# Seven block products of a pair of chunks, 512 columns each, in three single banks

## The chip, the cores and the metric

One core of a Trainium2 chip runs the whole program. The metric is the device time of one launch in microseconds (us), as the median of several runs.

## The reference

```python
B, N, C = 4, 6080, 256                       # q, k, v: (B, N, C); d_ff = 2048
qn = q / (np.linalg.norm(q, axis=1, keepdims=True) + 1e-06)
kn = k / (np.linalg.norm(k, axis=1, keepdims=True) + 1e-06)
s = kn.transpose(0, 2, 1) @ qn / tau         # (B, 256, 256): attention over channels
s = s - s.max(-1, keepdims=True)
a = np.exp(s)
a /= a.sum(-1, keepdims=True) + 1e-09
x = (v @ a).reshape(B * N, C)                # 24320 tokens
h = x @ w_in                                 # 256 -> 2048
g = np.where(h > 0.0, h, np.exp(np.minimum(h, 0.0)) - 1.0)
out = g @ w_out                              # 2048 -> 256
```

The weights arrive as float64; v and the output are stored with channels first.

## The kernel before

Since `(v a) w_in = v (a w_in)`, the kernel works out `a w_in` (256 x 2048) once per batch and multiplies the columns of v (tokens) by it. Every factor of a matmul is held as two fp32r tiles, a high part ("hi", a rounded copy) and a low part ("lo", the exact value minus hi), and a product is three matmuls: hi x hi, hi x lo, lo x hi. A batch has 12 chunks of tokens, 8 of 512 columns and 4 of 496.

Batch 0 runs in an older loop (one matmul set per 128 rows of h, `h_item`, `elu`, `out_item`). Beside it batch 1 is prepared. From chunk 12 (`NB`) on, which is the stretch of the change, the work goes in 144 units `(c, fq)`: chunk c and a quarter fq of the 2048 rows of h (512 rows). A unit multiplies a 2 x 2 block matrix A (the quarter of `a w_in`) by the 2 x 2 block matrix B (the chunk of v: two halves of the channels by two halves of the columns) with seven products instead of eight (Winograd's form). The sums of A blocks (S1 to S4) are made once per batch and quarter (`plan_s`), the sums of B blocks (T1 to T4) once per chunk (`t_sum`, `t_hi`, `t_lo`; `b_hi` and `b_lo` for the plain blocks B11, B21, B22). `product` issues one of the seven: both halves j of 128 rows, 3 matmuls each, 256 (or 248) columns, both halves into one PSUM bank of 512 columns.

In a unit PE goes: A11 x B11 into bank_a; S3 x T3 into bank_e; S2 x T2, later S1 x T1 and S4 x B22 into bank_b, on top of what lies there; A12 x B21 on top of bank_a; A22 x T4 on top of bank_e. Between them ACT copies bank_a into bank_b and bank_e into an SBUF tile p7, and DVE adds bank_b to p7, once into bank_e and once into p7. So four quads of h come about (e11 in bank_a, e21 in bank_e, e22 in p7, e12 in bank_b). For each of them ACT does Relu and Exp (`relu_exp`, L1183 and L1184), DVE a maximum (`largest`, L1187), the hi part goes out by a rounding DMA of POOL's queue (`hi_part`, L1204; for e12 by ACT, L1202), and in the next unit DVE makes the lo part (`lo_parts`, L1210 and L1212). With these parts `multiply_out` does the second product: three matmuls of the chunk's columns (L1127 to L1129, "out matmuls") for each half of the 256 output rows, added up in two po banks over the chunk's 16 row blocks, one or two units later. `copy_out` has ACT copy a full po bank and SP store it.

bank_a and bank_e come from a ring of three PSUM banks, bank_b is a fixed one, two banks are po, and two ("gram") hold what is prepared for the next batch.

From batch 2 on, the preparation of the batch runs beside the units, in small tasks: rows of q and k are loaded by SP, hi parts come by DMA from POOL, lo parts by DVE, squares by ACT, a DMA of POOL adds the squares up (acc), and PE adds to the channel product q, k ("gram", two matmuls a row and half, L203 and L210, one after each out matmul). Then follow norms, softmax, `a w_in` and the S sums.

The order on all five engines is written out: PE, ACT, DVE, POOL and SP are on a manual schedule, and each instruction waits for semaphores in its queue's order. Tasks sit in lists by engine and level. At fixed places of a unit, `spend(engine, budget, now)` takes ready tasks from these lists until their costs, in us, have used the budget; a task is ready when its time `when` (4 steps a unit) has come and what it needs lies some steps back (`late`, `GAP`).

Of the kernel before, what the change touches and what calls it, by code (L numbers as in the profile page):

```python
# [54 lines left out]
def channel_attention_then_elu_ffn(ctx: ExitStack, tc, q, k, vT, tau, w_in, w_out, outT):  # L55
# [33 lines left out]
    WB = 3  # L89
# [105 lines left out]
    def gram_item(hl, gram, ct, first, last):  # L195
# [6 lines left out]
        for r in range(2):  # L202
# [13 lines left out]
            )  # L216

# [554 lines left out]

# [16 lines left out]
    def new_s(fq):  # L789
        s_tiles[fq] = work.tile([P, 2, SPARE + 1, HF], F32R, tag="wp", bufs=2 * KT, name=f"s_{fq}")  # L790
# [54 lines left out]
    s_tiles = {}  # L845
# [104 lines left out]
    queues = {(e, level): [] for e in (ACT, DVE, POOL, PE, SP) for level in range(-2, 4)}  # L950
    GAP = {ACT: 0, DVE: 0, POOL: 2, PE: 2, SP: 0}

    class Task:
# [14 lines left out]
    def task(engine, cost, fn, deps=(), when=0, level=1, late=None):  # L968
# [3 lines left out]
        t.cost = cost  # L972
# [3 lines left out]
    def spend(engine, budget, now):  # L976
        for level in range(-2, 4):
            queue = queues[engine, level]
            while True:
# [7 lines left out]
                t.done = now  # L987

# [32 lines left out]
    def t_sum(c, k):
        hn = half_of(c)
        if k == 0:
            state["tt", c] = work.tile([P, 4, HF], F32, tag="raw", bufs=5, name=f"tt_{c}")
        v = vraw[c][:, :, 0 : 2 * hn].rearrange("p k (x t) -> p k x t", x=2)
        tt = state["tt", c][:, :, 0:hn]
        (
            lambda: nc.vector.tensor_sub(tt[:, 0:2], v[:, :, 1], v[:, 0]),
            lambda: nc.vector.tensor_add(tt[:, 2], tt[:, 1], v[:, 0, 0]),
            lambda: nc.vector.tensor_sub(tt[:, 3], v[:, 1, 0], tt[:, 2]),  # L1030
        )[k]()

# [4 lines left out]
    def t_lo(c, k):
        hn = half_of(c)
        t = t_groups[c % 2][:, k : k + 2]
        nc.vector.tensor_sub(t[:, :, 1, 0:hn], state["tt", c][:, k : k + 2, 0:hn], t[:, :, 0, 0:hn].bitcast(F32))  # L1040
        for y in range(2):
            operands[c, TERMS[k + y]] = t[:, y]

    TERMS = ("T1", "T3", "T2", "T4")

    BLOCKS = (("B11", 0, 0), ("B21", 1, 0), ("B22", 1, 1))

    def block_of(c, k):
        name, kt, x = BLOCKS[k]
        hn = half_of(c)  # L1050
        ring = (3 * (c - NB) + k) % FQ
        return s_tiles[ring][:, :, SPARE], vraw[c][:, kt, x * hn : (x + 1) * hn], hn, name

    def b_hi(c, k):
        to, _, hn, _ = block_of(c, k)
        _, kt, x = BLOCKS[k]
        t0 = span(c)[1] + x * hn
        nc.gpsimd.dma_start(to[:, 0, 0:hn], vT[kt * P : kt * P + P, t0 : t0 + hn])

    def b_lo(c, k):  # L1060
        to, src, hn, name = block_of(c, k)
        nc.vector.tensor_sub(to[:, 1, 0:hn], src, to[:, 0, 0:hn].bitcast(F32))
        operands[c, name] = to
# [527 lines left out]
```

## Time and profile before

| | |
|---|---|
| median of 3 runs | 2115.5 us (2113.42 to 2115.95) |
| the profiled execution's own time | 2112.71 us |
| its span, first to last instruction | 2110.9 us |
| PE busy | 2099.6 us, 99% of the span |
| DVE busy | 1594.0 us, 76% |
| ACT busy | 1475.1 us, 70% |
| POOL busy | 394.9 us, 19% |
| granted TensorE clock | 1.0 of full speed throughout |

In the rows of the timeline the columns are start and duration in us, engine, line, operation, out<-in, shape and count; in groups they are the busy time in us, the mean duration in ns, and the idle time of the engine just before, with what ended it. A row of waits reads: engine and instruction that waited, what it waited for, us in total, times, longest. Rows of windows have for each engine the busy time and count, then granted clock, DMA share and GB/s. Busy times of PE overlap: a matmul's duration goes past the start of the next one.

### The profile page before, as it was taken

To read this page: it belongs to the slowest core of one execution; us is meant where nothing else is said; L and a number is where in the kernel's file an instruction comes from. 1 tells how busy PE (TensorE), PEld (TensorE's weight loads), DVE (VectorE), ACT (ScalarE), POOL (GpSimd) and SP (SyncE) were. 2 spreads that over 40 slices of the span, in tenths; PEclk is the share of its full clock that TensorE was granted. 3 is DMA by queue.
4 is the path that set the end of the run, shared out by engine and by line. 5 is a ranking of instruction groups with operands and counts; after the bars stand their busy time and mean duration, and the time that the engine had idled before them with its cause. 6 is when DMAs were issued, how large, how long until landed. Compare 5 with 4: busy or idle time off the path is not lost. (4 is left out here: it accounts for less than half of the span.)

```text
span 2110.9 us, 35013 instructions
## 1 busy us (share of the span) xinstructions
PE 2099.6 (99%) x12833; PEld 1932.3 (92%) x12833; DVE 1594.0 (76%) x2428; ACT 1475.1 (70%) x2524; POOL 394.9 (19%) x715
## 2 busy tenths in 40 slices
PE   9999999999999999999999999999999999999999
PEld 8888888899889999999999999999999999999998
DVE  7988677777877777777778777777877877777775
ACT  6887776767776776777667767667766766766765
POOL 0000000000013333322122333332222221122211
PEclk9999999999999999999999999999999999999999
DMA  9320222220358787854456887876445443433432
GB/s 355 121 80 26 77 70 70 70 70 30 112 167 225 217 223 209 237 157 132 127 181 209 224 217 214 227 206 173 134 139 175 141 122 105 129 117 105 129 100 95
DMA packets 163371, 312.27 MB, mean 148 GB/s; under 512 B 17408, under 2 KB 59520, under 8 KB 161664
## 3 DMA queue, kind: packets, MB, share of 16 engines
q0 software_dynamic: 101376, 191.00, 32.8%
q1 hardware_dynamic: 61680, 118.91, 17.0%
q8 instruction: 102, 1.67, 0.3%
q14 instruction: 69, 0.57, 0.1%
q10 hardware_dynamic: 144, 0.13, 0.0%
HBM read 134.33 MB, written 31.20 MB: 78 GB/s over the span
## 5 line engine op out<-in xcount | busy, mean ns | idle before, releaser
L1127 PE MATMUL po<-g,wo 128*128 128x512 f32 (+1 forms) x1158 | 438.9, 379 | 0.0
L1129 PE MATMUL po<-g,wo 128*128 128x512 f32 (+1 forms) x1158 | 437.0, 377 | 0.0
L1128 PE MATMUL po<-g,wo 128*128 128x512 f32 (+1 forms) x1158 | 437.0, 377 | 0.0
L1204 POOL DMA_DIRECT2D g<-held x288 | 154.5, 536 | 930.4 <-DVE held L1187 511.9
L1183 ACT ACTIVATE held<-bank_a 128x512 f32<-128x512 f32 (+1 forms) x144 | 85.3, 592 | 324.3 <-PE po L1128 131.5
L1184 ACT ACTIVATE held<-held 128x512 f32<-128x512 f32 (+1 forms) x432 | 270.5, 626 | 13.8
L1212 DVE TENSOR_TENSOR g<-held,g 128x1024 fp32r<-128x1024 f32 (+1 forms) x216 | 260.3, 1205 | 24.1 <-DMA g<-held 24.1
L1104 PEld LDWEIGHTS bank_b<-t,s 128*128 128x128 f32 x1728 | 234.7, 191 | 24.8 <-ACT bank_b L1497 10.0
L1104 PE MATMUL bank_b<-t,s 128*128 128x256 f32 (+1 forms) x1728 | 240.6, 275 | 6.2 <-ACT bank_b L1497 5.8
L1129 PEld LDWEIGHTS po<-g,wo 128*128 128x128 f32 x1158 | 218.9, 189 | 28.9 <-DVE g L1212 0.5
L1104 PE MATMUL bank_e<-t,s 128*128 128x256 f32 (+1 forms) x1728 | 240.0, 275 | 0.0
L1128 PEld LDWEIGHTS po<-g,wo 128*128 128x128 f32 x1158 | 220.2, 190 | 17.3
L1127 PEld LDWEIGHTS po<-g,wo 128*128 128x128 f32 x1158 | 220.7, 191 | 13.0
L1505 DVE TENSOR_TENSOR bank_e<-bank_b,p 128x512 f32<-128x512 f32 (+1 forms) x144 | 99.7, 692 | 154.6 <-PE bank_b L1104 75.2
L1104 PEld LDWEIGHTS bank_e<-t,s 128*128 128x128 f32 x1728 | 216.1, 192 | 0.0
L1513 DVE TENSOR_TENSOR p<-bank_b,p 128x512 f32<-128x512 f32 (+1 forms) x144 | 98.8, 686 | 112.7 <-PE bank_b L1104 112.6
L1104 PE MATMUL bank_a<-s,s 128*128 128x256 f32 (+1 forms) x1296 | 179.8, 275 | 0.0
L1104 PEld LDWEIGHTS bank_a<-s,s 128*128 128x128 f32 x1296 | 168.2, 192 | 4.6
L114 ACT CAST g<-e 128x512 fp32r<-128x512 f32 (+1 forms) x192 | 116.7, 608 | 70.8 <-DVE e L447 39.4
L115 DVE TENSOR_TENSOR g<-e,g 128x512 fp32r<-128x512 f32 (+1 forms) x192 | 131.2, 683 | 46.2 <-ACT g L114 44.8
L474 PE MATMUL po<-g,wo 128*128 128x512 f32 (+1 forms) x378 | 142.7, 377 | 0.0
L472 PE MATMUL po<-g,wo 128*128 128x512 f32 (+1 forms) x378 | 142.6, 377 | 0.0
(228 smaller groups left out, 4344.9 us busy)
## 6 DMA issues: line engine op xcount, KB each, us to landing
g<-held POOLq DMA_DIRECT2D x192, 256.0 KB, 2.7
g<-other POOLq DMA_DIRECT2D x96, 256.0 KB, 3.8
g<-held POOLq DMA_DIRECT2D x96, 248.0 KB, 2.2
acc<-sq POOLq DMA_DIRECT2D x46, 512.0 KB, 5.0
raw<-in_q_dram SPq DMA_DIRECT2D x76, 256.0 KB, 4.9
raw<-in_k_dram SPq DMA_DIRECT2D x76, 256.0 KB, 5.3
v<-in_v_dram SPq DMA_DIRECT2D x32, 512.0 KB, 4.7
out_dram<-o SPq DMA_DIRECT2D x56, 256.0 KB, 2.0
```

Of the source, the lines that this page charges most:

```text
L114: nc.scalar.copy(hi, src)
L115: nc.vector.tensor_sub(lo, src, hi.bitcast(F32))
L472: nc.tensor.matmul(o, wo[:, f, 1, ds], hi, start=False, stop=False)
L474: nc.tensor.matmul(o, wo[:, f, 0, ds], lo, start=False, stop=last(c, f))
L1104: nc.tensor.matmul(bank[:, j, 0:hn], w[:, x, js], y, start=(begin and j == 0 and k == 0), stop=(j == 1 and k == 2), skip_group_check=True,)
L1127: yield nc.tensor.matmul(o, wo[:, f, 0, ds], hi, start=begin, stop=False)
L1128: yield nc.tensor.matmul(o, wo[:, f, 1, ds], hi, start=False, stop=False)
L1129: yield nc.tensor.matmul(o, wo[:, f, 0, ds], lo, start=False, stop=end)
L1184: nc.scalar.activation(e, e, AF.Exp, scale=-1.0)
L1204: nc.gpsimd.dma_start(to, e)
L1212: nc.vector.tensor_sub(lo, held[:, row, :, 0 : 2 * hn], hi.bitcast(F32))
L1505: nc.vector.tensor_add(ve, vb, vp)
```

## The change

A unit is now `(p, fq, j)`: a pair p of chunks, a quarter fq, and one of the two 128-row halves j of each A block. The two column halves of B are the two chunks of the pair. So a product is three matmuls of 512 (or 496) columns in one bank, and a unit makes 256 rows of h for two chunks where it made 512 rows for one. The number of units, 18 x 4 x 2 = 144, is as before, and so are the number of quads in a unit (four of 512 columns) and of out matmuls (24).

```diff
-    def product(bank, c, fq, a, t, begin=False):
-        hn = half_of(c)
-        w, m = s_tiles[fq][:, :, MATRICES.index(a)], operands[c, t]
-        hi, lo = (in_turns(m[:, x, 0:hn]) for x in range(2))
-        for j in range(2):
-            js = slice(j * P, j * P + P)
-            for k, (x, y) in enumerate(((0, hi), (0, lo), (1, hi))):
-                nc.tensor.matmul(bank[:, j, 0:hn], w[:, x, js], y, ...)
+    def product(bank, p, fq, j, a, t, begin=False):
+        n = columns(p)[1]
+        w = s_tiles[fq][:, :, MATRICES.index(a), j * P : j * P + P]
+        hi, lo = (in_turns(x[:, 0:n]) for x in operands[p, t])
+        for k, (x, y) in enumerate(((0, hi), (0, lo), (1, hi))):
+            nc.tensor.matmul(bank[:, 0:n], w[:, x], y, start=(begin and k == 0), stop=(k == 2), skip_group_check=True)
+        if (fq, j) == (FQ - 1, 1):
+            room.extend(operands.pop((p, t)))
...
+    bank_a, bank_e = (ps.tile([P, CH], F32, tag="w", bufs=WB, name=f"bank_{x}") for x in "ae")
...
+    PACE = PERIOD * 25 / NG          # was PERIOD * 30 / NG
...
+        product(bank_a, p, fq, j, "A11", "B11", True)
+        nc.scalar.copy(vb, va)
+        used = spend(DVE, 2.7, now)
+        spend(POOL, 3.9, now)
+        product(bank_e, p, fq, j, "S3", "T3", True)
+        nc.scalar.copy(vp, ve)
+        multiply_out(1, now)
+        spend(ACT, -0.3 if turn else 1.1, now)
+        product(bank_b, p, fq, j, "S2", "T2")
+        nc.vector.tensor_add(ve, vb, vp)
+        if before is not None:
+            before[0]()
+        product(bank_a, p, fq, j, "A12", "B21")
+        e11 = new_quad(u, 0, 0)
+        relu_exp(e11, va)
+        multiply_out(1, now + 1)
+        product(bank_e, p, fq, j, "A22", "T4")
+        e21 = new_quad(u, 1, 0)
+        relu_exp(e21, ve)
+        spend(ACT, -0.3, now + 1)
+        largest(e11, va)
+        hi_part(u, 0, 0)
+        product(bank_b, p, fq, j, "S1", "T1")
+        nc.vector.tensor_add(vp, vb, vp)
+        multiply_out(2, now + 1)
...
+        largest(e21, ve)
+        hi_part(u, 1, 0)
+        if before is not None:
+            before[1]()
+        product(bank_b, p, fq, j, "S4", "B22")
+        e12 = new_quad(u, 0, 1)
+        relu_exp(e12, vb)
...
+        multiply_out(2, now + 2)
+        if not turn:
+            largest(e22, vp)
+            hi_part(u, 1, 1)
+        multiply_out(2, now + 3)
+        largest(e12, vb)
+        hi_part(u, 0, 1)
...
+        used += spend(DVE, min(0.3, 3.0 - used), now + 3)
+        spend(ACT, 0.6 if turn else 1.7, now + 3)
```

`before[0]` and `before[1]` are the lo parts of the unit before (`lo_parts`, rows 1 and 0, two DVE instructions each). `turn` is the second unit of a pair, in which ACT copies out the four po banks of the pair before.

The rest, in words. PSUM: bank_a, bank_b and bank_e are fixed banks; four banks are po (two chunks, two halves of the output rows), and one is left for gram, so what is prepared for a batch takes turns in it. All hi parts of quads go by POOL's DMA. The exact v of a pair lies in two tiles; the T sums are made in them in place, and the full po banks are copied into them before the next pair is loaded. The 14 operand tiles of a pair (seven terms, hi and lo) come from a stock of 20: those of the B blocks of the next pair are made early, those of its T terms in the last unit of a pair, when the tiles of the old pair come free (`hi_of` on ACT, `lo_of` on DVE). ACT's and DVE's tasks are taken by due time instead of by level, with due tasks allowed over the budget. Rows of q and k go in halves (256 KB transfers), 24 groups over 25 units' steps instead of 30; gram takes three matmuls of 256 columns (hi x hi, hi x lo, lo x hi) where it took one of 512 and one of 256. The norms are summed per channel in columns and spread by one matmul.

How the instructions stand on PE, at the start of a unit near the end of the program (bank_a, bank_e and bank_b as above, po the out matmuls, g, t and s operand tiles). Before:

```order
L1104 MATMUL bank_a<-s_4777,s_4971 128x248 x6
L1104 MATMUL bank_e<-t_4716,s_4971 128x248 x6
L1127 MATMUL po_0_18812<-g_5161,wo 128x496
L1128 MATMUL po_0_18812<-g_5161,wo 128x496
L1129 MATMUL po_0_18812<-g_5224,wo 128x496
L1127 MATMUL po_0_18812<-g_5161,wo 128x496
L1128 MATMUL po_0_18812<-g_5161,wo 128x496
L1129 MATMUL po_0_18812<-g_5224,wo 128x496
L1104 MATMUL bank_b<-t_4716,s_4971 128x248 x6
```

Now, at the same place:

```order
L1145 MATMUL bank_a<-t_5047,s_5105 128x496
L1145 MATMUL bank_a<-t_more,s_5105 128x496
L1145 MATMUL bank_a<-t_5047,s_5105 128x496
L1145 MATMUL bank_e<-g_5177,s_5105 128x496
L1145 MATMUL bank_e<-t_4718,s_5105 128x496
L1145 MATMUL bank_e<-g_5177,s_5105 128x496
L1155 MATMUL po_0_5229<-g_5177,wo 128x496
L1156 MATMUL po_0_5229<-g_5177,wo 128x496
L1157 MATMUL po_0_5229<-g_5108,wo 128x496
L1145 MATMUL bank_b<-t_5047,s_5105 128x496
L1145 MATMUL bank_b<-g_5253,s_5105 128x496
L1145 MATMUL bank_b<-t_5047,s_5105 128x496
```

Three long matmuls stand for six short ones, and one set of out matmuls instead of two stands between S3 and S2, which waits for ACT's copy into bank_b.

On ACT, around that copy (L1497 before, L1567 now), where other and held are tiles of quads. Before:

```order
L1183 ACTIVATE held<-bank_b 128x496
L1184 ACTIVATE held<-held 128x496
L1183 ACTIVATE other_5092<-bank_e 128x496
L1184 ACTIVATE other_5092<-other_5092 128x496
L1202 CAST g_5249<-held 128x496
L1497 COPY bank_b<-bank_a 128x2x248
L1499 COPY p_5094<-bank_e 128x2x248
```

Now:

```order
L1219 ACTIVATE held<-bank_e 128x512
L1220 ACTIVATE held<-held 128x512
L1219 ACTIVATE held<-p_5100 128x512
L1220 ACTIVATE held<-held 128x512
L1219 ACTIVATE other_5103<-bank_b 128x512
L1220 ACTIVATE other_5103<-other_5103 128x512
L1567 COPY bank_b<-bank_a 128x512
L1571 COPY p_5100<-bank_e 128x512
```

Before the copy stood e12 (bank_b), e21 (bank_e) and a cast; now it is e12 alone, with e21 and e22 earlier.

On DVE, a unit from one sum into bank_e (L1505 before, L1575 now) on; p is p7, g the hi and lo parts. Before:

```order
L1505 TENSOR_TENSOR bank_e<-bank_b,p_5094 128x2x248
L1212 TENSOR_TENSOR g_5224<-held,g_5249 128x2x496
L1513 TENSOR_TENSOR p_5094<-bank_b,p_5094 128x2x248
L1187 SCALAR_TENSOR_TENSOR held<-held,bank_a 128x496
L1210 TENSOR_TENSOR g_5224<-other_5092,g_5249 128x496
L1210 TENSOR_TENSOR g_5224<-other_5093,g_5249 128x496
L1187 SCALAR_TENSOR_TENSOR held<-held,p_5094 128x496
```

Now:

```order
L1575 TENSOR_TENSOR bank_e<-bank_b,p_5100 128x512
L1244 TENSOR_TENSOR g_5108<-held,g_5177 128x512
L1244 TENSOR_TENSOR g_5108<-held,t_5107 128x512
L1223 SCALAR_TENSOR_TENSOR other_5104<-other_5104,bank_a 128x512
L1590 TENSOR_TENSOR p_5100<-bank_b,p_5100 128x512
L1223 SCALAR_TENSOR_TENSOR held<-held,bank_e 128x512
L1244 TENSOR_TENSOR g_5108<-other_5102,g_5177 128x512
L1244 TENSOR_TENSOR g_5108<-other_5103,t_5107 128x512
```

The lo parts of row 1 (L1244), which wait for POOL's DMAs, and the maximum of e11 (L1223) now stand ahead of the sum into p7 (L1590); there was one lo part (L1212, of row 0) before.

More of the change, by code (lines that the diff above doesn't have):

```diff
@@ L216, in gram_item, with gram_items @@
             )
+    def gram_items(hl, gram, ct, first, last):
+        cs = slice(ct * P, ct * P + P)
+        for r in range(2):
+            for k, (x, y) in enumerate(((0, 0), (0, 1), (1, 0))):
+                yield nc.tensor.matmul(
+                    gram[:, ct, :],
+                    hl[:, x, 1, r, cs],
+                    in_turns(hl[:, y, 0, r, :]),
+                    start=(first and ct == 0 and r == 0 and k == 0),
+                    stop=(last and r == 1 and k == 2),
+                    skip_group_check=True,
+                )
     def keep_warm(n):
@@ L976, in spend @@
     def spend(engine, budget, now):
-        for level in range(-2, 4):
+        whole = budget
+        if engine in (ACT, DVE):
+            queue = queues[engine, 0]
+            while True:
+                able = [t for t in queue if t.ready(now) and (t.cost <= budget + 0.3 or t.due < (0 if engine == DVE else -15))]
+                if not able:
+                    return whole - budget
+                t = min(able, key=lambda t: t.due)
+                queue.remove(t)
+                budget -= t.cost
+                t.fn()
+                t.done = now
+        for level in range(-4, 4):
             queue = queues[engine, level]
@@ L1037, in t_lo @@
[L1037 to L1052, printed above, removed]
@@ L1330, in plan_rows @@
+            los = [task(DVE, 1.22, lo, ready, due=t + 4 + 4.8 * g, late=3 if n == 2 else 0)]
+            for y, (square, add) in enumerate(squares):
+                s = task(ACT, 0.57, square, [*los, *([] if g else [prior.get("pw")])], due=t + 4 + 4.8 * g, late=0)
+                added[g, y] = task(POOL, 0.55, add, [s], level=1, late=1) if g else s
             for ct in range(KT):
@@ L1420, in plan_soft @@
-        for cost, fn in ((0.3, guarded), *turns[0], *refining, *turns[1], (0.2, taken)):
-            x = task(DVE, cost, fn, [x], level=0, late=1)
+            n["dg"] = tiny.tile([P, KT, P], F32, tag="y", bufs=1, name="dg")
+            for jt in range(KT):
+                nc.vector.tensor_scalar(n["dg"][:, jt], ident, n["ry"][:, 2 * jt : 2 * jt + 1], None, op0=ALU.mult)
+        x = task(DVE, 0.7, inverted, [x], due=t + 150, late=1)
+        x = task(DVE, 0.5, taken, [x], due=t + 150, late=1)
@@ L1519, in channel_attention_then_elu_ffn @@
-        product(bank_e, c, fq, "A22", "T4")
-        if before is not None:
-            before[2]()
-        relu_exp(e22, vp)
-        largest(e22, vp)
-        hi_part(u, 1, 1, hn)
-        relu_exp(e12, vb)
-        relu_exp(e21, ve)
-        largest(e12, vb)
-        hi_part(u, 0, 1, hn, True)
-        multiply_out(2, now + 2)
-        spend(DVE, 1.4, now + 2)
-        spend(ACT, 0.4, now + 2)
-        spend(POOL, 3.3, now + 2)
-        spend(SP, 1, now + 2)
-        def finish(e21=e21, ve=ve, u=u, hn=hn):
-            largest(e21, ve)
-            hi_part(u, 1, 0, hn)
```

573 lines of the change are left out of this document (308 added, 265 removed).

## The prediction

> **What bounds the kernel now.** I read the page's first lines, then the PE's waits, then the PE in order of time in the last quarter, where nothing but the products and the out matmuls run.
>
> ```profile
> PE 2099.6 (99%) x12833; PEld 1932.3 (92%) x12833; DVE 1594.0 (76%) x2428; ACT 1475.1 (70%) x2524; POOL 394.9 (19%) x715
> PE bank_b L1104 <- ACT bank_b L1497: 5.8, 10, 2.0
> PE bank_b L1104 <- DVE bank_e L1505: 0.4, 2, 0.2
> ```
>
> PE is busy for 99% of the span and waits in the unit stretch 12 times, 6.2 us in all. So time can only go by fewer or shorter matmul slots on PE, and can come back only by new waits of PE. A matmul's busy time overlaps the next one's, so its cost is read from starts. First a unit of a chunk of 512 columns, then one of 496:
>
> ```profile
> 1760.38 0.38 PE L1127 MATMUL po<-g,wo 128*128 128x512 f32 x1
> ...
> 1763.64 0.83 PE L1104 MATMUL bank_b<-s,s 128*128 128x256 f32 x6
> 1764.31 0.83 PE L1104 MATMUL bank_e<-t,s 128*128 128x256 f32 x6
> 1764.98 0.38 PE L1127 MATMUL po<-g,wo 128*128 128x512 f32 x1
> ...
> 1766.28 0.83 PE L1104 MATMUL bank_a<-s,s 128*128 128x256 f32 x6
> ...
> 1768.91 0.83 PE L1104 MATMUL bank_b<-t,s 128*128 128x256 f32 x6
> ...
> 1770.25 0.38 PE L1127 MATMUL po<-g,wo 128*128 128x512 f32 x1
> ```
>
> ```profile
> 2040.02 0.38 PE L1127 MATMUL po<-g,wo 128*128 128x496 f32 x1
> ...
> 2041.28 0.83 PE L1104 MATMUL bank_a<-s 128*128 128x248 f32 x6
> 2041.94 0.83 PE L1104 MATMUL bank_e<-t,s 128*128 128x248 f32 x6
> 2042.61 0.38 PE L1127 MATMUL po<-g,wo 128*128 128x496 f32 x1
> ...
> 2049.73 0.38 PE L1127 MATMUL po<-g,wo 128*128 128x496 f32 x1
> ```
>
> Twelve product matmuls of 256 columns take 1764.98 - 1763.64 = 1.34 us, 111.7 ns each. The unit takes 1770.25 - 1760.38 = 9.87 us and holds 42 of them and 24 out matmuls, so one of 512 columns takes (9.87 - 42 x 0.1117) / 24 = 215.8 ns. With 496 columns: 12 products of 248 take 1.33 us, 110.8 ns each; the unit takes 9.71 us, an out matmul (9.71 - 42 x 0.1108) / 24 = 210.6 ns. A product matmul of 248 columns thus costs nearly what one of 256 does, while the long ones scale with their columns: in a row of short ones something beside the columns takes a share.
>
> **The change, part by part.**
>
> *Products.* 42 short matmuls a unit become 21 long ones with the same columns; there are 144 units before and after, 96 of 512 columns and 48 of 496. 512: 42 x 111.7 - 21 x 215.8 = 4691 - 4532 = 0.16 us a unit, 15.3 us. 496: 42 x 110.8 - 21 x 210.6 = 4654 - 4423 = 0.23 us, 11.1 us. Together -26.4 us, all of it on PE, which is the path.
>
> [...]
>
> *Gram matmuls.* For batches 2 and 3 (24 groups x 2 halves x 2 rows x 2 batches = 192 places) one of 512 and one of 256 columns become three of 256, each between two out matmuls:
>
> ```profile
> 1203.70 0.38 PE L203 MATMUL gram<-qk 128*128 128x512 f32 x1
> 1203.91 0.38 PE L1128 MATMUL po<-g,wo 128*128 128x512 f32 x1
> 1204.13 0.27 PE L210 MATMUL gram<-qk 128*128 128x256 f32 x1
> 1204.24 0.38 PE L1129 MATMUL po<-g,wo 128*128 128x512 f32 x1
> ```
>
> 0.21 + 0.11 us become 3 x 0.11: at most +0.01 us, +1.0 us over 192 places (bounds 0 and +2). The norms' and softmax's matmuls change by a handful; nothing is put down for them.
>
> *The waits that stand now.* Where ACT comes late with its copy into bank_b, PE stands:
>
> ```profile
> 1003.47 0.37 PE L1129 MATMUL po<-g,wo 128*128 128x496 f32 x1
> 1003.87 0.56 ACT L1497 COPY bank_b<-bank_a 128x496 f32<-128x496 f32 x1
> 1004.48 0.93 PE L1104 MATMUL bank_b<-t,s 128*128 128x248 f32 x6 [0.64 <-ACT bank_b L1497]
> ```
>
> S2 would have started at 1003.68 and started 0.80 us later, against 0.64 shown as idle; so the 6.2 us cost about 6.2 x 0.80 / 0.64 = 7.8 us. Why ACT is late is seen in a unit without a wait: A11 starts at 1766.28 and ends 0.83 later, at 1767.11, yet the copy starts at 1768.05, because the two steps of e12 and of e21 and a cast stand ahead of it in ACT's queue. In the new order the last product, S4, ends 2.6 us ahead of the next A11, and the cast of e12 goes to POOL's queue; so I take 3 of the 7.8 us to stay (the start of the stretch, where ACT and DVE still finish the old loop).
>
> *The walk through a new unit.* Each bank now serves one product at a time, and one out matmul set (0.65 us) instead of two stands behind A11 and S3. Durations:
>
> ```profile
> L1497 ACT COPY bank_b<-bank_a 128x512 f32<-128x512 f32 x96 | 55.4, 577 | 10.6 <-PE bank_a L1104 10.6
> L1183 ACT ACTIVATE held<-bank_a 128x512 f32<-128x512 f32 x96 | 57.3, 597 | 192.8 <-PE po L1128 99.5 <-DVE g L1212 44.8 <-PE po L1129 31.7
> L1184 ACT ACTIVATE held<-held 128x512 f32<-128x512 f32 x288 | 181.6, 631 | 9.2
> L1505 DVE TENSOR_TENSOR bank_e<-bank_b,p 128x512 f32<-128x512 f32 x96 | 67.0, 698 | 105.6 <-issue 43.0 <-PE bank_b L1104 42.2 <-ACT sq L1295 18.5
> L1210 DVE TENSOR_TENSOR g<-other,g 128x512 fp32r<-128x512 f32 x96 | 61.9, 686 | 8.7 <-DMA g<-other 8.7
> L1212 DVE TENSOR_TENSOR g<-held,g 128x1024 fp32r<-128x1024 f32 (+1 forms) x216 | 260.3, 1205 | 24.1 <-DMA g<-held 24.1
> 1769.84 0.70 DVE L1505 TENSOR_TENSOR bank_e<-bank_b,p 128x512 f32<-128x512 f32 x1 [0.97 <-PE bank_b L1104]
> ```
>
> From a matmul set's end DVE starts 0.1 us later (1768.91 + 0.83 to 1769.84), and PE starts 0.05 after ACT's copy (1003.87 + 0.56 to 1004.48). Count from A11's start, 0.216 us a matmul, last one ending 0.38 after its start.
> - A11 ends at 0.81. The copy into bank_b runs 0.86 to 1.44. S2 is due at 1.94: 0.45 to spare (PE passes 3 + 3 + 3 matmuls). In the old order it was due at 2.64.
> - S2 ends at 2.75; DVE's sum into bank_e runs 2.85 to 3.55. A22 is due at 18 x 0.216 = 3.89: 0.3 to spare.
> - On DVE there follow two lo parts (to 4.9) and the maximum of e11 (to 5.6); S1 ends at 5.35, so the sum into p7 runs 5.6 to 6.3. S4 is due at 6.48: 0.1 to 0.3 to spare.
> - S4 ends at 7.3; ACT's two steps of e12 end at 8.6 and DVE's maximum at 9.3. ACT then has up to 2.0 us of side work before the next copy at 9.72 + 0.86 = 10.6, DVE up to 2.7 us before its next sum at 12.6. Both just fit.
> So in a plain unit PE waits for nothing, and the margins are a few tenths. ACT's work a unit is 8 x 0.61 + 2 x 0.58 = 6.0 us and DVE's 10 x 0.69 = 6.9 us of 9.72, before side work.
>
> *Where it does not fit.* (a) The second unit of each pair (17 of them): ACT also copies four po banks out (4 x 0.58), e22 moves behind e12, DVE's last maximum ends near 10.6, and with 2.7 us of side work its sum ends at 4.0 instead of 3.55, 0.1 late; bounds 0 and 0.6 us, I take 0.2: +3.4 us. The casts of the T terms stand in the last unit of a pair: T3's lo part ends about 0.3 after the next A11's start, and S3's second matmul is due at 0.86; hidden. (b) The row stretches. The row groups of a batch are spread over 25 units' steps instead of 30, and four e parts a unit go out by DMA instead of three.
>
> ```profile
> 600.00:800.00 200.00, 197.87 (x1321) 184.40 (x1320) 150.10 (x227) 143.06 (x242) 63.60 (x111) 1.00 0.78 215
> 1700.00:2110.00 410.00, 407.23 (x2724) 382.31 (x2723) 290.59 (x425) 273.91 (x489) 80.32 (x152) 1.00 0.37 113
> g<-held POOLq DMA_DIRECT2D x192, 256.0 KB, 2.7
> g<-other POOLq DMA_DIRECT2D x96, 256.0 KB, 3.8
> qk<-in_k_dram POOLq DMA_DIRECT2D x46, 256.0 KB, 6.3
> ```
>
> These windows end with the granted clock, the DMA share and GB/s: 0.78 and 215 there, 0.37 and 113 in the last batch. A unit in a row stretch moves about 215 GB/s x 10.8 us = 2.3 MB, of which three e parts are 0.8. A fourth adds 0.26; rows 1.2 times as dense add at most 0.2 x 1.5 = 0.3. The share so becomes 0.78 x 2.56 / 2.3 = 0.87 to 0.78 x 2.86 / 2.3 = 0.97 (estimate), close to full. The e22 part is issued near 8.9 of a unit of 11 us (out matmuls with gram between them) and its lo part stands ahead of the sum into p7, due near 4.4 of the next: 6.5 us for a transfer whose median is 2.7 to 3.8, and 6.3 for the longest kind. I take one in ten of the 50 units to be 0.8 us late: +4 us; bounds 0 and 50 x 1 = 50 us. POOL itself issues 8 to 10 transfers of 0.53 us a unit; no bound.
>
> *First pair.* Its 7 terms are cut up in the old loop, some 4 us more of DVE work over 13 steps of 2.5 us, beside 12 matmuls a step: nothing.
>
> *Sum.* 2112.7 us is the profiled execution (span 2110.9 and 1.8 around it). 2112.7 - 26.4 + 1.0 + (3 + 3.4 + 4 - 7.8 = +2.6) = 2089.9. The median of the runs shown, 2115.5, stands 2.8 above the profiled one, so 2093.
>
> **The rivals.**
> - *Slower: the lo parts wait for their DMAs.* DVE's queue is in order, so a late e21 or e22 holds back the maximum of e11 and the sum into p7, and S4 behind them; bank_b is single, so PE has nothing to take instead. For it: the share of 0.9 and the tenths of margin. Against it: in the old kernel DVE's lo parts waited for these transfers 8.7 + 24.1 = 33 us over 144 units and PE stood for 0.4 us of DVE's. It decides from 0.5 us a unit over 50 units, which takes back 25 us; at 1 us, 2093 - 4 + 50 = 2139 us, slower.
> - *No change that can be told: PE's gain goes into small waits everywhere.* If the sum into p7 comes 0.15 us late in all 144 units (its margin is 0.1 to 0.3), 22 us go: 2115.
> - *The fixed share of a matmul is smaller than the products' row says.* Gram's short one between two long ones takes 0.11 us (1204.13 to 1204.24). If the long products lost half of what the short ones lose in a row, a pair would save 2 x 110 - 215.8 = 4 ns: 3024 x 4 = 13 us instead of 26, and 2106. Against it: the out matmuls, which also change weights each time, run at 215.8. [...]
> - *Fewer waits than now*: the 10.4 us put down come out at 0: 2083.
>
> **How the numbers follow.** My forecast with the last rival as its lower end (2076 to 2105): 0.72. Its gain partly taken, by DMA waits, by small waits or by slower long products (2105 to 2118): 0.14, of which the last has 0.04. Slower by DMA waits (over 2118): 0.14. A change under 0.2% (4.2 us) can hardly be told in this kernel. Faster (under 2111.3): 0.72 and 0.06 of the second case, 0.78; same: its other 0.08; slower 0.14. The range, 2076 to 2118, leaves out 0.04 below (of the 0.72) and 0.14 above; its lower end is 2112.7 - 26.4 - 7.8 with the runs' scatter of 2 us.
>
> **What would show it.** Right: a unit of the last batch takes 45 x 0.2158 = 9.71 us (512) and 9.48 (496); the PE's waits name bank_b or bank_e and stay under 12 us; PE stays at 99%. Wrong: a unit in the last batch over 9.8 us (a margin that is negative, or long products slower than out matmuls); PE waits of tens of us released by DVE's sum into p7 between 600 and 900 or 1200 and 1500, with DVE waiting for g's DMAs there.

## The result and the profile after

The changed kernel takes 2120.7 us (median of 11 runs, 2114.2 to 2125.6) against 2114.5 for the kernel before (11 runs on the same chip, 2113.0 to 2116.0). The ratio is 1.0027, with a 95% interval of 1.0016 to 1.0038: slower by a little. The prediction, 2093 us (2076 to 2118) and faster, was wrong. The profiled execution shown here took 2121.8 us, with a span of 2120.0; in it the granted clock is 0.996 on average, against 1.00 before. One of the eleven runs of turn_undone, below, was a slow one (2930 us at a granted clock of 0.70), which its ratio leaves out.

The page's first lines and its software DMA queue, of the kernel after:

```profile
PE 2087.5 (98%) x10009; PEld 1843.0 (87%) x10009; DVE 1590.8 (75%) x2498; ACT 1446.3 (68%) x2428; POOL 484.8 (23%) x853
...
q0 software_dynamic: 120960, 228.36, 38.0%
```

PE has 12 us less of busy time, and yet the span is 9 us longer: PE now stands. Its waits, as before:

```profile
PE bank_b L1145 <- DVE p L1590: 13.7, 10, 2.8
PE bank_e L1145 <- DVE bank_e L1575: 7.1, 8, 1.1
PE gram L223 <- DVE qk L1350: 3.3, 5, 0.7
PE bank_b L1145 <- ACT bank_b L1567: 1.3, 1, 1.3
```

ACT's late copy into bank_b, which led this list before, is down from 5.8 us to 1.3. DVE's two sums now lead it. In the last batch the unit is what the prediction said. Here are the first matmuls of A11 in two following units of 512 columns, and of S4 in two of 496:

```profile
1802.27 0.38 PE L1145 MATMUL bank_a<-t,s 128*128 128x512 f32 x1
...
1811.98 0.38 PE L1145 MATMUL bank_a<-t,s 128*128 128x512 f32 x1
...
2048.90 0.79 PE L1145 MATMUL bank_b<-s,s 128*128 128x496 f32 x3
...
2058.31 0.79 PE L1145 MATMUL bank_b<-s,s 128*128 128x496 f32 x3
```

9.71 us instead of 9.87, and 9.41 instead of 9.71. So the products are faster, and the time goes elsewhere. To say where, I count PE's lost time in each profile: what lies between the starts of two matmuls beyond 0.216 us (512 columns), 0.209 (496) or 0.110 (256), in single stalls of over some 0.15 us, from the start of the unit stretch on. It is 8.2 us before and 40.9 after. Span less lost time is 2102.7 before and 2079.1 after: 23.6 us won, 32.7 lost again.

The lost time is not spread out. With u the number of the unit (0 to 143), a pair of chunks takes eight units, and u mod 8 = 1 is the turn unit. Of the 40.9 us, 13.2 lie in units with u mod 8 = 2, 14.8 in those with u mod 8 = 4 (nearly all of it in the row stretches), 7.5 in five stretches of half clock (a granted clock of 0.50 for 3.413 us each), and 3.4 at the start of the unit stretch, as before.

**The unit after the turn.** The chain of waits in unit 50, in order of time (start, us, what):

```profile
1135.49 6.09 DMA t<-other
...
1141.68 0.10 DVE g L1244
...
1142.29 0.68 DVE held L1223
1142.96 0.61 DVE p L1590
...
1143.62 1.65 PE bank_b L1145 x3
```

The transfer is the hi part of e22, which the turn unit issues last. It takes 6.09 us, where the page's row of such transfers gives a median of 2.3 (the second row is needed below), and five other transfers are issued within 2 us of it. It is not alone: over the turn units 9 to 105 e22's transfer takes 4.6 us in the median, and the last hi part of the other units 2.2 to 2.8. The rows of the page (transfer, count, KB each, median us from issue to landing):

```profile
t<-other POOLq DMA_DIRECT2D x144, 256.0 KB, 2.3
...
acc<-raw POOLq DMA_DIRECT2D x92, 256.0 KB, 4.7
```

POOL's queue behind it:

```profile
1136.01 0.55 POOL L1374 DMA_DIRECT2D qk<-in_q_dram  x1
...
1137.05 0.57 POOL L1083 DMA_DIRECT2D g<-in_v_dram  x1
```

SP's load of the next pair of v, and DVE's wait:

```profile
1136.35 1.04 SPq L1067 DMA_DIRECT2D exact<-in_v_dram  x2
...
1141.68 0.69 DVE L1244 TENSOR_TENSOR g<-other,t 128x512 fp32r<-128x512 f32 x1 [3.36 <-DMA t<-other]
```

DVE reaches the lo part 2.8 us after the issue of the transfer and stands there 3.36 us; the maximum of e11, the sum into p7 and PE's S4 stand behind it.

**The units with u mod 8 = 4.** In unit 12, in a row stretch, POOL's queue:

```profile
714.53 1.86 POOL L1383 DMA_DIRECT2D acc<-raw  x2
719.59 0.86 POOL L1383 DMA_DIRECT2D acc<-raw  x1 [3.19 <-ACT held L1220]
720.12 0.90 POOL L1374 DMA_DIRECT2D qk<-in_q_dram  x1
```

DVE's rows behind it:

```profile
726.52 1.23 DVE L1350 TENSOR_TENSOR qk<-raw,qk 128x1024 fp32r<-128x1024 f32 x1 [3.85 <-DMA qk<-in_k_dram]
727.66 0.68 DVE L1091 TENSOR_TENSOR t<-exact,s 128x512 fp32r<-128x512 f32 x1
728.26 0.68 DVE L1091 TENSOR_TENSOR t<-exact,t 128x512 fp32r<-128x512 f32 x1
728.86 0.69 DVE L1575 TENSOR_TENSOR bank_e<-bank_b,p 128x512 f32<-128x512 f32 x1
```

And PE's:

```profile
727.80 0.38 PE L223 MATMUL gram<-qk 128*128 128x256 f32 x1 [0.66 <-DVE qk L1350]
...
729.61 0.48 PE L1145 MATMUL bank_e<-t,s 128*128 128x512 f32 x1 [1.11 <-DVE bank_e L1575]
```

POOL issues the two adds of a group at 714.53 and then stands until 719.59 with the first add of the next group: it adds into the same half of acc, so the earlier add must have landed (a median of 4.7 us for these, in the row above), and the square by ACT that it needs had been done since 707.5 (the row names a later instruction of ACT). The casts of rows and of e parts queue behind it, the row's lo part on DVE waits 3.85 us for them, and behind that stand two more of DVE's tasks (lo parts of v's blocks, L1091) and the sum that PE's A22 needs.

That POOL stands there for the landing shows in two further views. First, POOL's own waits for semaphores at the add (count; shortest, median and longest in ns) in the kernel before, where a group had one add of 512 KB, in the kernel after, and in add_gap, an experiment below:

```profile
L1298 POOLq EVENT_SEMAPHORE  x46: 17/42/43, 632.7 to 1453.7; - x46
...
L1383 POOLq EVENT_SEMAPHORE  x83: 17/17/5118, 635.9 to 1456.5; - x83
...
L1383 POOLq EVENT_SEMAPHORE  x86: 17/17/43, 636.9 to 1466.7; - x86
```

In the kernel after, six of these waits last 4.1 to 5.1 us, one ahead of the stall in each of the units 12, 20, 28, 60, 68 and 76, and all others 43 ns at most. The one of unit 12 ends at 719.10; the earlier add, issued at 714.53, landed at 719.07. Second, in unit 28 the row itself names the landing:

```profile
902.45 0.87 POOL L1383 DMA_DIRECT2D acc<-raw  x1 [5.32 <-DMA acc<-raw]
```

### The profile page after: what moved, and what is told of

Read it like the earlier page. It is cut to its first block, busy times and chain, and to the rows that moved or that the text cites. A ratio compares the mean times of both kernels' runs of the same rounds, so it can differ in the third digit from the quotient of the medians.

```text
span 2120.0 us, 29468 instructions
## 1 busy us (share of the span) xinstructions
PE 2087.5 (98%) x10009; PEld 1843.0 (87%) x10009; DVE 1590.8 (75%) x2498; ACT 1446.3 (68%) x2428; POOL 484.8 (23%) x853
## 4 chain that ended last, share of the span: by engine, by line
PE 89%; DMA 4%; DVE 3%; ACT 2%; issue 2%; POOL 0%; DVEq 0%; POOLq 0%
PE bank_b L1145 12%; PE po L1156 10%; PE po L1157 10%; PE po L1155 10%; PE bank_e L1145 8%; PE bank_a L1145 8%; PE ph L444 4%; PE ph L445 4%; PE ph L446 4%; PE po L488 4%; PE po L486 4%; PE po L484 4%; PE gram L223 3%; PE gram L572 2%; DMA t<-other 2%
## 5 line engine op out<-in xcount | busy, mean ns | idle before, releaser
L1157 PE MATMUL po<-g,wo 128*128 128x512 f32 (+1 forms) x1158 | 439.6, 380 | 0.0
L1156 PE MATMUL po<-t,wo 128*128 128x512 f32 (+1 forms) x792 | 300.9, 380 | 0.0
L1155 PE MATMUL po<-t,wo 128*128 128x512 f32 (+1 forms) x792 | 300.5, 379 | 0.0
L1575 DVE TENSOR_TENSOR bank_e<-bank_b,p 128x512 f32<-128x512 f32 (+1 forms) x144 | 99.8, 693 | 252.9 <-PE bank_b L1145 246.4
L1567 ACT COPY bank_b<-bank_a 128x512 f32<-128x512 f32 (+1 forms) x144 | 81.5, 566 | 244.0 <-PE bank_a L1145 236.2
L1157 PEld LDWEIGHTS po<-g,wo 128*128 128x128 f32 x1158 | 220.2, 190 | 28.8 <-issue 0.2
L1220 ACT ACTIVATE other<-other 128x512 f32<-128x512 f32 (+1 forms) x325 | 203.7, 627 | 10.3
L1237 POOL DMA_DIRECT2D t<-other x217 | 117.1, 540 | 398.5 <-DVE other L1223 198.9
L1145 PE MATMUL bank_b<-t,s 128*128 128x512 f32 (+1 forms) x528 | 182.9, 381 | 7.6 <-DVE p L1590 7.6
L1155 PEld LDWEIGHTS po<-t,wo 128*128 128x128 f32 x792 | 150.9, 190 | 19.9
L1156 PEld LDWEIGHTS po<-t,wo 128*128 128x128 f32 x792 | 150.5, 190 | 18.9
L223 PE MATMUL gram<-qk 128*128 128x256 f32 x576 | 159.0, 276 | 4.6 <-DVE qk L1350 3.3
L1220 ACT ACTIVATE held<-held 128x512 f32<-128x512 f32 (+1 forms) x251 | 157.6, 628 | 8.0
L1244 DVE TENSOR_TENSOR g<-other,t 128x512 fp32r<-128x512 f32 (+1 forms) x217 | 144.7, 680 | 19.7 <-DMA t<-other 19.6
L488 PE MATMUL po<-g,wo 128*128 128x512 f32 (+1 forms) x378 | 142.7, 377 | 0.0
L486 PE MATMUL po<-g,wo 128*128 128x512 f32 (+1 forms) x378 | 142.6, 377 | 0.0
L484 PE MATMUL po<-g,wo 128*128 128x512 f32 (+1 forms) x378 | 142.6, 377 | 0.0
L1156 PE MATMUL po<-g,wo 128*128 128x512 f32 (+1 forms) x366 | 139.3, 381 | 0.0
L1155 PE MATMUL po<-g,wo 128*128 128x512 f32 (+1 forms) x366 | 138.9, 380 | 0.0
```

What stands on the lines that cost most here:

```text
L223: yield nc.tensor.matmul(gram[:, ct, :], hl[:, x, 1, r, cs], in_turns(hl[:, y, 0, r, :]), start=(first and ct == 0 and r == 0 and k == 0), ...
L484: nc.tensor.matmul(o, wo[:, f, 0, ds], hi, start=first(c, f), stop=False)
L486: nc.tensor.matmul(o, wo[:, f, 1, ds], hi, start=False, stop=False)
L488: nc.tensor.matmul(o, wo[:, f, 0, ds], lo, start=False, stop=last(c, f))
L1145: nc.tensor.matmul(bank[:, 0:n], w[:, x], y, start=(begin and k == 0), stop=(k == 2), skip_group_check=True)
L1155: yield nc.tensor.matmul(o, wo[:, f, 0, ds], hi, start=begin, stop=False)
```

## The experiments

The theory: the products gain what was forecast; two fixed places in the in-order queues of POOL and DVE take it back, and PE's stalls there bring stretches of half clock on top. The rivals: the DMA's load as such, through the denser rows and the fourth transfer of a unit; and the single banks with ACT's copies.

All kernels are edits of the changed one. Lost time and its parts are counted as above, each in the profiled run; medians and ratios are against the kernel before on the same chip.

| kernel | median us | ratio, 95% interval | span | lost | u mod 8 = 2 | u mod 8 = 4 | half clock |
|---|---|---|---|---|---|---|---|
| after | 2120.7 | 1.0016 to 1.0038 | 2120.0 | 40.9 | 13.2 | 14.8 | 7.5 |
| lo_order | 2107.4 | 0.9959 to 0.9982 | 2106.0 | 27.8 | 1.3 | 13.8 | 4.3 |
| turn_undone | 2112.4 | 0.9983 to 1.0000 | 2109.5 | 31.6 | 3.2 | 14.2 | 5.9 |
| add_gap | 2115.8 | 1.0002 to 1.0020 | 2114.0 | 35.9 | 13.7 | 7.5 | 5.3 |
| both | 2104.1 | 0.9935 to 0.9968 | 2107.8 | 30.1 | 6.4 | 7.8 | 4.9 |
| rows_last | 2122.0 | 1.0029 to 1.0056 | 2118.9 | 39.8 | 2.3 | 19.2 | 4.9 |
| three | 2091.2 | 0.9890 to 0.9917 | 2087.6 | 11.7 | 2.0 | 0.3 | 0 |
| four | 2093.0 | 0.9891 to 0.9919 | 2087.4 | 11.0 | 0 | 0 | 0 |
| add_rows | 2103.0 | 0.9943 to 0.9972 | 2099.7 | 21.3 | 10.7 | 0 | 1.6 |
| rows_slower | 2127.2 | 1.0048 to 1.0079 | 2125.7 | 47.3 | 2.0 | 23.8 | 5.6 |
| e12_by_act | 2116.2 | 1.0004 to 1.0023 | 2115.6 | 36.2 | 7.8 | 6.5 | 3.4 |

Span less lost time lies between 2075.9 and 2079.4 us in all eleven. So what tells these kernels apart is PE's lost time alone. The start of the stretch, 3.4 us in each, waits of pw and single stalls in other units make up the rest of a row. The kernels were measured in four rounds, in which the kernel before had medians of 2114.5, 2113.7, 2113.0 and 2113.1 us, so differences of medians across rounds are good to about 1 us. The profiled run of both is the slowest of its six (2109.5 us), so its row shows more lost time than its median would.

**lo_order**: the order of DVE's lo parts in the unit after a turn.

```
-        if before is not None:
-            before[0]()
+        turned = u > 2 and u % 8 == 2
+        if turned:
+            lo_parts(u - 1, 1, (0,))          # e21
+        elif before is not None:
+            before[0]()
...
         nc.vector.tensor_add(vp, vb, vp)      # the sum into p7
+        if turned:
+            lo_parts(u - 1, 0, (0,))          # e11
...
+        if turned:
+            lo_parts(u - 1, 0, (1,)); lo_parts(u - 1, 1, (1,))   # e12, e22
+        elif before is not None:
+            before[1]()
```

> Changed kernel with one edit: in the unit after a turn unit (u mod 8 = 2) DVE takes the lo parts in the order in which their hi parts were issued, e21, e11, e12, e22, and only the one of e21 stands ahead of the sum into p7. Theory (the e22 transfer that the turn unit issues last holds DVE's queue): the 13 us of PE's idle time in these units go, and with them two of the five clock drops (1.5 us each), so 2120.7 - 16 = 2105 us, and units with u mod 8 = 4 still stand some 15 us. Rival (transfers are late everywhere because the DMA is loaded): the wait only moves to another lo part and to the out matmuls, over 2116 us.

Measured 2107.4 us, 13.3 less than the changed kernel, as the theory said. PE's waits for the sum into p7, 13.7 us before the edit:

```profile
PE bank_b L1145 <- DVE p L1593: 3.7, 4, 2.5
```

e22's transfers of the turn units land as late as before the edit (4.6 us in the median in both), and still the stalls behind them fall from 13.2 to 1.3 us. So the lateness of a transfer, whatever load it comes from, costs nothing here until something that PE needs stands behind it.

**turn_undone**: e22 ahead of e12 again in turn units.

```
-        if not turn:        # e22's steps on ACT and DVE
+        if not swap:        # swap = False; likewise `if swap` for `if turn`
```

> Changed kernel with one part of the change undone: in turn units e22 stands ahead of e12 again, as in other units (the smaller budgets of ACT there stay). Theory (the place of e22's transfer at the end of the turn unit): it is issued about 1.2 us earlier, stalls of 2 to 3 us shrink to 1 to 2 us, 13 us become 4 and two clock drops go: about 2109 us. Rival (contention with the load of the next pair of v, which begins there in either order): within 3 us of 2120.7. Second rival (ACT's copies of the output banks make the sum into p7 or bank_b late in the turn unit itself): slower, 2125 us.

Measured 2112.4 us, 8.3 less than the changed kernel. The stalls after the turn fall from 13.2 to 3.2 us, as forecast, so the place of e22's steps at the end of the unit brings them; the load of the next pair, which is the same here, is not enough by itself. Those with u mod 8 = 4 stand, and one stretch of half clock went instead of two.

**add_gap**: an add is ready only two steps after the one before into the same half.

```
-                added[g, y] = task(POOL, 0.55, add, [s], level=1, late=1) if g else s
+                added[g, y] = task(POOL, 0.55, add, [s, *([(added[g - 1, y], 2)] if g > 1 else [])], level=1, late=1) if g else s
```

The step count of such a dependency is taken as told, also within one engine.

> Changed kernel with one edit: an add of squares into acc on POOL's queue becomes ready only two steps after the add of the group before into the same half, so that POOL's queue does not stand at it. Theory (POOL stands for the landing of the earlier add, and the transfers behind it, the casts of rows and of e parts, are issued late): the 15 us of PE's idle time in units with u mod 8 = 4 of the row stretches go, with three of five clock drops, so 2120.7 - 19 = 2102 us. Rival (the rows' transfers are late because of the DMA's load, whatever the order on POOL): the waits stay within a third, over 2115 us.

Measured 2115.8 us: 4.9 won where 19 were forecast. Of its waits:

```profile
PE bank_e L1145 <- DVE bank_e L1575: 7.4, 9, 1.1
PE gram L223 <- DVE qk L1350: 0.6, 2, 0.4
PE pw L818 <- DMA wi<-wi_scr: 3.6, 4, 1.9
```

Gram's waits went, the ones at bank_e stayed, and pw's came. The stalls with u mod 8 = 4 fell by half, 14.8 to 7.5 us. POOL's long waits at the add are all gone (43 ns at most, in the view above). So POOL's standing is about half of the second place; that the rest is DVE's order was only a guess here. The intervals of this kernel and of the changed one overlap, so the 4.9 us of the medians are less sure than the fall of the stalls.

**both**: lo_order and add_gap together.

> Both edits together. Theory (two fixed places in the queues take back the gain, and the clock drops come from their stalls): PE's idle time returns to about 10 us and no clock drop is left, so 2120.7 - 33 = 2088 us, which would beat the kernel before by 1.2%. Rival (DMA load): over 2110 us, with new stalls elsewhere.

Measured 2104.1 us, neither the theory's 2088 nor the rival's 2110. At bank_e stand stalls of 1.2 to 1.3 us in units with u mod 8 = 4, in five of them, always with a row's lo part and two L1091 ahead of the sum. In unit 12 that lo part now waits 2.67 us for the load of its rows, which SP issues, and no longer for a cast of POOL. Half clock took another 4.9 us, and waits of pw 4.5.

**rows_last**: lo_order, and in units with u mod 8 = 4 the rows' lo parts only after the sum into p7.

```
-        used = spend(DVE, 2.7, now)
+        sums_first = u % 8 == 4
+        used = spend(DVE, 2.7, now, sums_first)       # then without rows' lo parts
...
         nc.vector.tensor_add(vp, vb, vp)
+        if sums_first:
+            used += spend(DVE, 1.4, now + 1)
```

(The expectation takes the two L1091 for sums of v's blocks; they are lo parts.)

> The kernel lo_order with one more edit: in units with u mod 8 = 4 DVE takes only the two sums of v's blocks (T terms) ahead of the sum into bank_e, and the lo part of the rows, which waits for its transfer, after the sum into p7. Theory (what is left there is DVE's order: a row's lo part that waits for its transfer, and two sums behind it, all ahead of the sum that PE needs): the stalls there, 15 us in lo_order, fall to 3 or less, with one or two clock drops: 2107.4 - 13 = 2094 us. Rival (POOL's blocked queue makes everything late there, the e parts too): only the 1.27 us at bank_e go, 2103 us, and stalls at bank_b take their place.

Measured 2122.0 us, 15 slower than lo_order. The theory fell for this edit alone, and the rival's mechanism is seen, at a higher price than the rival's 2103. POOL still waits up to 4.4 us at the add. DVE's row in unit 12:

```profile
729.21 0.69 DVE L1244 TENSOR_TENSOR g<-held,t 128x512 fp32r<-128x512 f32 x1 [2.46 <-DMA t<-held]
```

PE's waits for the sum into p7, 3.7 us in lo_order:

```profile
PE bank_b L1145 <- DVE p L1594: 19.8, 10, 3.6
```

POOL stands at the add, so the e parts are cast late as well. With the row's lo part out of the way DVE runs into e's next, and the stall moves from bank_e to bank_b.

**three**: lo_order, add_gap and rows_last together.

> The kernel both with the edit of rows_last. Theory: the eight stalls of 1.2 us at bank_e in units with u mod 8 = 4 and the gram stalls ahead of them (12 us together) go, with one clock drop: 2104 - 12 = 2092 us. Rival (each stall removed lets the next late transfer show): over 2100 us.

Measured 2091.2 us, 0.9904 of the kernel before (0.9890 to 0.9917): it beats the kernel before and the changed one. Two lines of the page:

```profile
PE 2074.0 (99%) x10009; PEld 1839.0 (88%) x10009; DVE 1589.2 (76%) x2498; ACT 1445.5 (69%) x2428; POOL 484.8 (23%) x853
...
q0 software_dynamic: 120960, 228.36, 38.5%
```

PE's waits for DVE's two sums:

```profile
PE bank_e L1145 <- DVE bank_e L1576: 4.3, 6, 1.4
PE bank_b L1145 <- DVE p L1594: 1.5, 3, 0.8
```

The same packets and bytes as in the changed kernel, at a higher rate, the same banks, and no stretch of half clock. The longest wait of POOL at the add is 43 ns. So neither the DMA's load nor the single banks cost this time by themselves; where the instructions stand in the queues decides it.

**four**: the rows' lo parts behind the sum into p7 also in units with u mod 8 = 2.

> As three, and the rows' lo parts also stand behind the sum into p7 in the units after a turn (u mod 8 = 2), where two of them came ahead of the sum into bank_e. Theory: another 4 us (stalls of 1.9, 1.2, 1.0 and 0.4 us at bank_e in both): 2088 us. Rival (the row lo parts then come later, and gram and the squares with them, and the soft part of the batch begins late): not under 2092 us.

Measured 2093.0 us, not to be told from three. The rival fits: 2.0 us of stalls went there, and two of 1.4 and 1.5 us came in units 13 and 21.

**add_rows**: three without lo_order.

> The kernel three without the edit of lo_order: the changed kernel with the add's gap on POOL's queue and the rows' lo parts behind the sum into p7 in units with u mod 8 = 4. Theory (two separate places, each with its own price): the stalls with u mod 8 = 4 are gone, those with u mod 8 = 2 stand at bank_b, released by the sum into p7, 13 us and two clock drops: 2091 + 15 = 2106 us. Rival (the places depend on each other: fewer stalls in the one place put the queues at ease in the other): under 2098 us.

Measured 2103.0 us, 11.9 above three: the first place has a price of its own, and it is nearly additive. The waits for the sum into p7:

```profile
PE bank_b L1145 <- DVE p L1591: 8.6, 7, 2.4
```

**rows_slower**: lo_order with `PACE = PERIOD * 30 / NG`.

> The kernel lo_order with the row groups of a batch spread over 30 units' steps, as in the kernel before, instead of 25. Theory (the adds and the lo parts pile up behind the turn unit, at whatever pace): the stalls with u mod 8 = 4 remain for the most part, 8 to 12 of 15 us: 2107.4 - 5 = 2102 us. Rival (the density of the rows' transfers, the prediction's own reason): under 5 us remain and no clock drop: 2094 us.

Measured 2127.2 us: slower than lo_order by 20 us, which both theories miss. Rows that come less densely did not help by themselves. In unit 76 two rows' lo parts now fell into one unit, ahead of the sum into bank_e, which starts at 1442.80:

```profile
1432.38 1.23 DVE L1350 TENSOR_TENSOR qk<-raw,qk 128x1024 fp32r<-128x1024 f32 x1 [1.93 <-DMA raw<-in_k_dram]
1441.66 1.23 DVE L1350 TENSOR_TENSOR qk<-raw,qk 128x1024 fp32r<-128x1024 f32 x1 [8.05 <-DMA raw<-in_k_dram]
```

The second waited 8 us for the load of its rows, whose place in SBUF, by the code, comes free only after an add on POOL's queue. PE stood 8.6 us there and 7.1 in unit 28. Again what PE waits for is a task that stands ahead of a sum. But the edit moves the rows' tasks to other units as well, so it does not tell what the density alone costs.

**e12_by_act**: ACT casts e12's hi part, as before the change.

```
-        hi_part(u, 0, 1)
+        hi_part(u, 0, 1, True)
```

> Changed kernel with one part of the change undone: the hi part of e12 is cast by ACT, as in the kernel before, and no longer by a transfer on POOL's queue. Each unit has one transfer of 256 KB and one POOL issue less, ACT 0.6 us more. Theory (places in the queues, not load): e22's transfer is still the last of a turn unit and the adds still block POOL; some stalls shrink, and ACT's copy into bank_b comes late in some units instead: within 6 us of 2120.7. Rival (the fourth transfer a unit fills the DMA): the stalls released by DVE fall by more than half, 2104 us or less.

Measured 2116.2 us, within the theory's range, but both sides moved:

```profile
PE bank_b L1145 <- ACT bank_b L1567: 10.3, 11, 2.0
PE bank_b L1145 <- DVE p L1590: 9.1, 10, 1.4
PE bank_e L1145 <- DVE bank_e L1575: 3.3, 5, 1.1
```

Waits for DVE fall from 24.1 us (with gram's) to 13.4, less than the rival's half, and ACT's late copy comes back, 10.3 us. So the fourth transfer does cost something, by its load or by its place in POOL's queue, which this run does not tell apart, and it buys the end of ACT's lateness.

**ladder**: lo_order with the last lo part repeated ahead of the sum into p7, in eight units of the last batch.

```
+        for _ in range(LADDER.get(u, 0)):     # {109: 2, 111: 3, 117: 4, 119: 5, 125: 6, 127: 7, 133: 9, 135: 12}
+            e, hi, lo = (y[:, 0:n] for y in quads[u - 1, 1, 1])
+            nc.vector.tensor_sub(lo, e, hi.bitcast(F32))
         nc.vector.tensor_add(vp, vb, vp)
```

> The kernel lo_order with a lo part of e22 written again 2, 3, 4, 5, 6, 7, 9 and 12 times ahead of the sum into p7, in eight separate units of the last batch (u = 109, 111, 117, 119, 125, 127, 133, 135), where no clock drop was seen. Each repetition is some 0.62 us of DVE, so PE's stalls should be about 1, 1.6, 2.2, 2.9, 3.5, 4.1, 5.3 and 7.2 us. Theory (a single PE stall of over about 2.2 us halves the granted clock for 3.4 us): no drop after the first two, a drop after those from 2.9 us on, and each costs 1.5 to 1.7 us beyond its stall; span 2106 + 28 + 6 x 1.6 = 2144 us. Rival (the drops go with the transfers and the row stretches, not with the stall): no drop at all here, 2134 us.

Measured in one run: a span of 2145.8 us, at a granted clock of 0.992 on average (0.997 in lo_order). PE's stalls were 0.93, 1.66, 2.38, 3.11, 3.83, 4.56, 5.90 and 8.03 us by the starts. The first three brought no drop of the clock, the other five did. The span came near the theory's 2144, though with five drops and not six. The windows' view, 3.41 us each, around the stall of 2.38 and the one of 3.11 (after PE, PEld, DVE, ACT and POOL: granted clock, DMA share, GB/s):

```profile
1842.19:1845.60 3.41, 2.35 (x11) 1.71 (x10) 3.31 (x6) 1.65 (x3) 0.53 (x1) 1.00 0.23 74
1845.60:1849.01 3.41, 2.25 (x10) 2.00 (x11) 3.41 (x6) 2.21 (x4) 0.53 (x1) 1.00 0.03 9
1849.01:1852.43 3.42, 3.42 (x17) 3.00 (x16) 0.78 (x2) 1.40 (x3) 1.06 (x2) 1.00 0.70 223
...
1866.08:1869.50 3.42, 0.47 (x3) 0.10 (x1) 3.32 (x6) 0.12 (x1) 0.22 (x1) 1.00 0.24 77
1869.50:1872.91 3.41, 3.41 (x8) 2.67 (x9) 2.84 (x5) 2.99 (x6) 0.53 (x1) 0.50 0.24 77
```

After the longer stall 8 matmuls go in 3.41 us, after the shorter one 17 in 3.42. Since no rows and no adds run there, PE's standing alone brought the drop there, and the rival falls.

## Why the prediction was wrong, point by point

- *Products, -26.4 us.* Right. The units came to 9.71 and 9.41 us (forecast 9.71 and 9.48), and span less lost time fell by 23.6 us, where products and gram together were to bring 25.4; the units of 496 won more than forecast. A unit gained 0.16 us (512) and 0.30 us (496). Gram's single matmuls of 256 columns between two long ones came at 109 ns by their starts in the kernel before (192 of them); only those in a row took 111.7.
- *The old waits, 3 of 7.8 us to stay.* Right: 3.4 us at the start of the stretch, and one late copy of ACT.
- *The walk through a plain unit.* Right: in the last batch units of 9.71 us follow each other without a wait.
- *(a) The turn unit, +3.4 us.* Wrong. I looked there for DVE's own work and found a tenth of a microsecond. The cost, 13.2 us, lies in the unit behind it and comes from a step that the change moved: e22's hi part, issued last, lands up to 6 us later. The allowance of 6.5 us was worked out for a unit in normal order; in unit 50 it was 2.8 us. The transfers issued beside it were not counted.
- *(b) The row stretches, +4 us.* Wrong in size and in kind: 14.8 us. "One in ten of the 50 units" took lateness as a chance; it is always the same unit, and there 2 to 3.6 us. "POOL itself issues 8 to 10 transfers ...; no bound" counted POOL's time per issue and not what stands ahead of an issue: 4 to 5 us behind an add that must land. That the adds now come two to a group, in halves, had no term at all.
- *The clock.* The sum has no term for it and gives no reason: 7.5 us in five stretches.
- *Sum.* 2089.9 + 9.8 (a) + 10.8 (b) + 7.5 (clock) + 1.8 (products and gram won less) = 2119.8 us, against 2121.8 for the profiled run.
- *The rival "Slower: the lo parts wait for their DMAs"* had the mechanism, DVE's queue behind a late transfer, with 25 us as the point from which it decides; the stalls in the two places are 28 us, in some 15 units at up to 3.6 us rather than in 50 at 0.5. Its chance of 0.14 rested on a row that did not say what I took from it. DVE waited 33 us for these transfers before the change (38 with the 5.6 us of L1210's group of 496 columns, which the prediction left out), and PE stood for 0.4. After the change it waits less for e's transfers, but the rows' lo parts have waits that they did not have: L1318, which made them before, stood 0.8 us in all, and for no DMA. The groups of the kernel after:

```profile
L1244 DVE TENSOR_TENSOR g<-other,t 128x512 fp32r<-128x512 f32 (+1 forms) x217 | 144.7, 680 | 19.7 <-DMA t<-other 19.6
L1244 DVE TENSOR_TENSOR g<-held,t 128x512 fp32r<-128x512 f32 (+1 forms) x179 | 120.1, 678 | 5.9 <-DMA t<-held 5.6 <-PE po L1156 0.3
L1350 DVE TENSOR_TENSOR qk<-raw,qk 128x1024 fp32r<-128x1024 f32 x48 | 58.4, 1221 | 27.7 <-DMA qk<-in_k_dram 20.5 <-DMA raw<-in_k_dram 7.0
```

25 us at e's lo parts, and PE pays for much of it behind the turn. What had hidden these waits was the slack behind DVE's sums, which the prediction itself had worked out to shrink to a few tenths; a wait that cost nothing under the old slack was no evidence under the new one. The 27.7 us at the rows' lo parts are new, and the kernel before had no row that could show them: 20.5 of them, in five units with u mod 8 = 4, are for casts that stand behind the add in POOL's queue. With the stalls of both places removed (kernel three) the time is 2091. That is near the forecast of 2093, but it is another kernel: the prediction had the products right and not the order of the queues.

## What to carry to other kernels

When a change shortens the bound engine's work and takes its slack away, list every wait of the engines beside it that the slack covered, and every new entry in a queue that must wait for a landing, and price each at its own place in the order: the unit in which a step was moved last, the queue entry that stands behind a landing. Follow a moved DMA to its landing and to the first in-order instruction that needs it, and keep off the path to the bound engine whatever may wait: order consumers as their data land. Fixes of two separate places were nearly additive here (lo_order won 13.3 us alone and 11.9 on top of the rest). Fixes within one place were not: the third edit here cost 15 us on top of the first (2107.4 to 2122.0) and won 13 on top of the first two (2104.1 to 2091.2).

## What the runs showed of the hardware

*Behind stalls of PE the granted clock was 0.50 for 3.41 us.* In the changed kernel, behind a stall of 2.44 us in unit 28 (same columns as above):

```profile
911.35:914.76 3.41, 1.25 (x6) 1.15 (x7) 3.41 (x7) 2.97 (x6) 0.70 (x2) 1.00 0.21 68
914.76:918.17 3.41, 3.41 (x10) 2.80 (x10) 3.24 (x5) 1.71 (x4) 0.36 (x1) 0.50 0.39 124
```

10 matmuls, where the same time at full clock has 17 (the ladder's third row above). From the start of the unit stretch on, this run has five such pieces, each 3.413 us long at a granted clock of 0.50, from 730.44, 914.76, 1143.45, 1256.09 and 1505.27 us on. They start 54, 67, 33 and 73 steps of 3.413 us apart, so on one grid. I took PE's standing time, by the starts of its matmuls, in each step of that grid over the same part of the run. It is longest in the five steps just ahead of the half clock: 2.25, 2.27, 2.81, 2.30 and 2.55 us. The next three, with 2.02, 1.99 and 1.76 us, were followed by full clock. So what counted here is how much of one step PE stood. The 2.25 us ahead of 730.44 hold no stall over 1.27; the stall of 2.38 us in the ladder lay across two steps (PE busy for 2.35 us of one and 2.25 of the next) and cost nothing more, and the one of 2.44 us here cost another 1.5 us. Counted from the first instruction, the grid lies elsewhere in another run: the ladder's half clock at 1869.50 starts 279.7 steps behind the one at 914.76 here. That fits the runs of the changed kernel, which scatter more than those of the kernel before: the fastest, 2114.2 us, had a granted clock of 0.999, the slowest, 2125.6, one of 0.995. That the place of the grid makes this scatter is a guess of mine and was not shown.

*POOL's issuing queue stood for a landing.* Where two adds into the same half of acc followed each other closely in POOL's queue, the queue waited at the second one's semaphore until the first had landed, 4.1 to 5.1 us in each of six places, and the casts of rows and of e parts behind it were issued late. With two steps between such adds (add_gap) no such wait is over 43 ns. The releaser that a row names can mislead here: in unit 12 it is ACT, in unit 28 the landing.
